# A decode block with cached attention: the first four key loads all in halves, and the projection's second part closed earlier

## The chip, the cores and the metric

One core of a Trainium2 chip runs the whole kernel. The metric is device time in microseconds (us) of that core. Differences here are below one per cent, so most kernels were timed in five or six runs, in alternation with the kernel before on the same chip.

## The reference

```python
xn  = layernorm(x)                              # x: 4 x 1 x 640, bf16
q   = (xn @ wq) per head                        # 32 heads of 128
p   = softmax(q k_cache^T * 128**-0.5)          # caches: 4 x 32 x 4096 x 128, bf16
att = (p v_cache, heads joined) @ wo            # wo: 4096 x 640
mlp = gated MLP of xn                           # w_in 640 x 1728, w_out 864 x 640
return x + att + mlp                            # 4 x 1 x 640
```

The two caches hold 268 MB and are read once. Everything else is small.

## The kernel before

The work is cut into 16 units: four groups of eight heads, times four batch rows. A unit has a K load and a V load of 8.39 MB each. The on-chip buffer has five slots of half a unit, so each load takes two neighbouring slots, and a load can be issued only when what lay there has been read. All large loads go through one queue, in order: K0 to K3, then V0, K4, V1, K5 and so on.

```python
seq = [("k", u) for u in range(B)]                       # B = 4
for u in range(NU):                                      # NU = 16
    seq.append(("v", u))
    if u + B < NU:
        seq.append(("k", u + B))
place = {("k", 0): 3, ("k", 1): 0, ("k", 2): 2, ("k", 3): 0}      # first slot of two
for u in range(B, NU):
    place[("k", u)] = 1 if u % 2 == 0 else 0
for u in range(NU):
    place[("v", u)] = 3
...
cuts = {("k", u): (0, T // 2, T) for u in range(NU) if u == 1 or u % B == B - 1}   # loaded in halves
cuts[("v", NU - 1)] = (0, 128, 192, 240, T)
first = {u: u % 2 for u in range(B, NU) if ("k", u) not in cuts}   # which half is read first
first[2] = 1
```

A K unit is transposed by VectorE in eight pieces, four a half, and multiplied with the queries by TensorE:

```python
hh = first.get(u, 0) ^ (k // 4)                           # half, k = 0..7
nc.vector.transpose(kT[:].rearrange("p (t r) -> p t r", r=32), kw)
... # 8 matmuls into S
```

After the fourth K of a group comes the softmax, then V matmuls of the group. The end of the kernel is the output projection. `proj` is one PSUM bank; even columns c of a group go to its lower rows, odd ones to rows 64 up, and the two parts are added at the end:

```python
odd = c % 2 == 1 and not (g == NG - 1 and c == HG - 1)
r0 = 64 * odd + 32 * hf
nc.tensor.matmul(proj[r0:r0 + B, 0:NO2], lhsT=oT[:, c, :], rhs=wo_t[g][:, c, ...],
                 start=False, stop=(g == NG - 1 and c in (HG - 3, HG - 1)))
...
emit_proj(NG - 1, range(0, HG - 2))
nc.vector.tensor_copy(out=o_1[:], in_=proj[64:128, 0:NO2])
emit_proj(NG - 1, range(HG - 2, HG))
nc.vector.tensor_tensor(out=o_bf[:], in0=proj[0:64, 0:NO2], in1=o_1[:], op=ALU.add)
```

## Time and profile before

| kernel before | |
|---|---|
| time of the three runs at hand for the prediction | 667.51 us median (667.27 to 668.79) |
| the run that was profiled | 668.32 us, span 666.5 |
| DMA over the span | 282.25 MB, 423 GB/s |
| busy: VectorE, TensorE, ScalarE | 54%, 45%, 12% |

The page and the trace's views are read in the prediction below. Two things to know for them: a line of the chain has start, duration and what ran; a line of the queue (SPq) shows when a load was issued, not when its data moved.

### The profile page before, as it was taken

The page shows a single profiled execution, that of the slowest core. Times are in us where ns is not written, and L with a number is a line of the kernel's source. Part 1 is how long each engine was busy: PE and PEld are TensorE (multiplying, and loading weights), DVE is VectorE, ACT ScalarE, POOL GpSimd, SP SyncE. Part 2 cuts the span into 40 slices and gives each one's busy share as a digit, 9 for nine tenths or more (in the row PEclk, how much of TensorE's full clock was granted, in tenths as well). Part 3 has the DMA queues.
Part 4 walks back from the last instruction along what each step waited for, and adds up shares of the span by engine and source line. Part 5 has one row for each costly group of instructions (what it writes and reads, how often), then busy time and mean ns, then how long its engine had stood idle before and what let it go on. Part 6 is the DMA issues. An engine that isn't in the chain of part 4 may idle for free.

```text
span 666.5 us, 5583 instructions
## 1 busy us (share of the span) xinstructions
PE 298.7 (45%) x2366; PEld 110.7 (17%) x2366; DVE 359.2 (54%) x340; ACT 82.7 (12%) x169; POOL 6.2 (1%) x24
## 2 busy tenths in 40 slices
PE   0516466266063446235336065643606254724164
PEld 0402121122021122111112022111202112211021
DVE  5339799555190749609246285735628084940002
ACT  0400000440200000440200000071010000053200
POOL 0000000000000000000000000000000000000000
PEclk9658968668677696766858677755857767667665
DMA  9999999999999999999999999999999999999995
GB/s 374 452 409 462 413 425 438 440 371 440 434 440 438 433 410 444 425 438 437 434 440 425 430 421 441 425 438 440 434 437 426 429 437 416 451 437 426 412 417 224
DMA packets 7381, 282.61 MB, mean 424 GB/s; under 512 B 840, under 2 KB 1212, under 8 KB 1724
## 3 DMA queue, kind: packets, MB, share of 16 engines
q1 hardware_dynamic: 7340, 282.25, 98.5%
q8 instruction: 18, 0.29, 0.2%
q14 instruction: 7, 0.06, 0.0%
q10 hardware_dynamic: 16, 0.01, 0.0%
HBM read 282.25 MB, written 0.01 MB: 423 GB/s over the span
## 4 chain that ended last, share of the span: by engine, by line
DMA 72%; DVE 12%; issue 12%; PE 2%; ACT 1%; SPq 1%; DVEq 0%; ACTq 0%
DMA kv<-in_A_k_cache_dram 64%; DVE kT L353 11%; DMA kv<-in_A_v_cache_dram 4%; DMA kv<-in_A_wo_dram 3%; PE O L435 2%; DVE xd L418 0%; ACT Zb L399 0%; PE S L364 0%; ACT p L407 0%; DVE pT L411 0%; DVE m L371 0%; SPq L152 0%; PE proj L476 0%; SPq L110 0%; PE misc L376 0%
## 5 line engine op out<-in xcount | busy, mean ns | idle before, releaser
L353 DVE STREAM_TRANSPOSE kT<-kv 128x2048 f32<-128x2048 f32 x128 | 282.7, 2277 | 127.2 <-DMA kv<-in_A_k_cache_dram 127.2
L364 PE MATMUL S<-kT,QZ 128*32 128x512 bf16 x1024 | 191.2, 507 | 231.2 <-DVE kT L353 231.2
L364 PEld LDWEIGHTS <-QZ 128*32 128x32 bf16 x1024 | 61.0, 112 | 355.7 <-issue 336.1
L435 PE MATMUL O<-kv,Zb 128*32 128x512 bf16 x1024 | 77.3, 467 | 62.0 <-ACT Zb L399 30.3
L442 DVE TENSOR_SCALAR R<-O,Mk 128x128 f32<-128x128 f32 x16 | 5.6, 351 | 130.8 <-PE O L435 130.8
L399 ACT ACTIVATE Zb<-xd,MkE 32x256 bf16<-32x256 bf16 x112 | 51.5, 499 | 107.2 <-PE O L435 105.8
L407 ACT ACTIVATE p<-S,negmax 128x512 bf16<-128x512 f32 x8 | 5.4, 683 | 402.0 <-DVE negmax L385 402.0
L435 PEld LDWEIGHTS <-Zb 128*32 128x32 bf16 x1024 | 33.2, 114 | 105.2 <-issue 61.5
L452 PE MATMUL misc<-R,SelR 128*32 128x128 f32 x32 | 6.6, 289 | 26.0 <-DVE R L444 26.0
L418 ACT COPY xd<-pT 32x256 bf16<-32x256 bf16 x28 | 17.2, 614 | 5.7 <-DVE pT L411 5.2
L444 DVE SCALAR_TENSOR_TENSOR R<-O,Mk,R 128x128 f32<-128x128 f32 x48 | 16.8, 351 | 1.7
L418 DVE COPY xd<-pT 32x256 bf16<-32x256 bf16 x36 | 13.1, 364 | 0.6
L340 POOL COPY QZ<-q 32x32 bf16<-32x32 bf16 x16 | 5.1, 320 | 424.3 <-PE S L364 398.3
L411 DVE STREAM_TRANSPOSE pT<-p 128x1024 bf16<-128x1024 bf16 x4 | 5.0, 1246 | 6.3 <-ACT p L407 6.3
L476 PE MATMUL proj<-kv,oT 128*4 128x320 bf16 x64 | 6.9, 453 | 2.5 <-DMA kv<-in_A_wo_dram 1.7
L371 DVE TENSOR_REDUCE m<-S 128x2 f32<-128x1024 f32 x4 | 4.9, 1224 | 5.7 <-PE S L364 5.7
L452 PEld LDWEIGHTS misc<-R,SelR 128*32 128x32 f32 x32 | 2.2, 109 | 33.5 <-DVE R L444 24.8
L256 DVE CAST kv<-q 128x512 bf16<-128x512 f32 x4 | 2.5, 684 | 8.4 <-PE q L248 8.4
L376 PE MATMUL misc<-dg,ones_f 128*128 128x256 f32 x8 | 3.6, 537 | 7.6 <-DVE dg L373 7.6
L455 DVE SCALAR_TENSOR_TENSOR om<-misc,rinv,MkH 32x1024 bf16<-32x1024 f32 x4 | 5.1, 1271 | 2.2 <-PE misc L452 2.2
L423 PE MATMUL misc<-rowsum,SelPe 128*32 128x1 f32 x16 | 2.1, 199 | 9.0 <-ACT p L407 9.0
L248 PE MATMUL q<-kv,xnT 128*32 128x512 bf16 x40 | 3.6, 533 | 5.0 <-DMA kv<-in_A_wq_dram 5.0
(94 smaller groups left out, 62.6 us busy)
## 6 DMA issues: line engine op xcount, KB each, us to landing
kv<-in_A_k_cache_dram SPq DMA_DIRECT2D x10, 4096.0 KB, 37.3
kv<-in_A_wq_dram SPq DMA_DIRECT2D x1, 5120.0 KB, 15.2
kv<-in_A_v_cache_dram SPq DMA_DIRECT2D x1, 4096.0 KB
kv<-in_A_wo_dram SPq DMA_DIRECT2D x3, 1280.0 KB, 19.0
kv<-in_B_w_in_dram SPq DMA_DIRECT2D x1, 2160.0 KB, 19.8
kv<-in_A_v_cache_dram SPq DMA_DIRECT2D x1, 2048.0 KB
kv<-in_A_v_cache_dram SPq DMA_DIRECT2D x1, 1536.0 KB
kv<-in_B_w_out_dram SPq DMA_DIRECT2D x1, 960.0 KB
```

Of the source, the lines that this page charges most:

```text
L340: nc.gpsimd.tensor_copy(out=QZ[r0:r0 + 32, :, :, :, 8 + 8 * hp], in_=q3[r0:r0 + 32, :, NE * hp:NE * hp + NE, g * B:g * B + B].rearrange("p ...
L353: nc.vector.transpose(kT[:].rearrange("p (t r) -> p t r", r=32), kw)
L364: nc.tensor.matmul(S_ps[32 * q:32 * q + 32, e], lhsT=QZ[:, b, 2 * kh + w, e, w0:w0 + 32], rhs=kb[:, i, :, e, :, w], start=(b == 0 and k < ...
L399: nc.scalar.activation(out=dst, in_=src, func=ACT.Copy, scale=mk)
L407: nc.scalar.activation(out=p_bf[:, :, e, :], in_=S_ps[:, e], func=ACT.Exp, bias=negmax[:, e:e + 1], scale=scale, accum_out=rowsum[:, e:e + 1])
L418: op(out=xd[32 * hp:32 * hp + 32, :, q, :], in_=pT[32 * q:32 * q + 32, :, hp, :].rearrange("p t x -> p x t"))
L435: nc.tensor.matmul(O_ps[32 * q:32 * q + 32, :, :], lhsT=Zb[b % 2][:, w].rearrange("p h c -> p (h c)"), rhs=vv[:, w * 4 * Dh:(w + 1) * 4 * ...
L442: nc.vector.tensor_scalar(out=R, in0=O_ps[:, 0, :], scalar1=Mk4[:, 0:1], scalar2=None, op0=ALU.mult)
L444: nc.vector.scalar_tensor_tensor(out=R, in0=O_ps[:, c, :], scalar=Mk4[:, c:c + 1], in1=R, op0=ALU.mult, op1=ALU.add)
L452: nc.tensor.matmul(oh[:], lhsT=SelR[:, b].rearrange("p h b -> p (h b)"), rhs=state["R"][:, b, :], start=(b == 0), stop=(b == B - 1))
L455: nc.vector.scalar_tensor_tensor(out=om[:], in0=oh[:, None, :].to_broadcast((G, HG, Dh)), scalar=state.pop(("rinv", g))[:, 0:1], in1=MkH[: ...
L476: nc.tensor.matmul(proj[r0:r0 + B, 0:NO2], lhsT=oT[:, c, :], rhs=wo_t[g][:, c, hf * NO2:(hf + 1) * NO2], start=False, stop=(g == NG - 1 an ...
```

## The change

Its intent: VectorE can start on the first half of K0 sooner, K2 need not land whole, and so the slots of the first group are freed sooner. At the end, the copy of the odd part is taken out of the last matmuls' way by closing that part after column 3.

```diff
-    cuts = {("k", u): (0, T // 2, T) for u in range(NU) if u == 1 or u % B == B - 1}
+    cuts = {("k", u): (0, T // 2, T) for u in range(NU) if u < B or u % B == B - 1}
...
-    first[2] = 1
...
-                odd = c % 2 == 1 and not (g == NG - 1 and c == HG - 1)
+                odd = c % 2 == 1 and not (g == NG - 1 and c >= HG // 2)
...
-                                 start=False, stop=(g == NG - 1 and c in (HG - 3, HG - 1)))
+                                 start=False, stop=(g == NG - 1 and c in (HG // 2 - 1, HG - 1)))
...
-    emit_proj(NG - 1, range(0, HG - 2))
+    emit_proj(NG - 1, range(0, HG // 2))
...
-    emit_proj(NG - 1, range(HG - 2, HG))
+    emit_proj(NG - 1, range(HG // 2, HG))
```

## The prediction

> **What bounds the kernel now.** I first read the page's slices, to see which engine never rests.
>
> ```profile
> DMA  9999999999999999999999999999999999999995
> GB/s 374 452 409 462 413 425 438 440 371 440 434 440 438 433 410 444 425 438 437 434 440 425 430 421 441 425 438 440 434 437 426 429 437 416 451 437 426 412 417 224
> ```
>
> The 16 DMA engines are busy in every slice until the last, and the page has 282.25 MB read in 666.5 us, 423 GB/s. VectorE is busy 54% and TensorE 45%. So only three things can shorten the run: fewer holes in the stream of loads, a shorter start before it or a shorter tail after it. The ninth slice (133 to 150 us) shows 371 GB/s between neighbours at 440: a hole. The first slice is the start-up. A single slice can be off by a few packets that are counted where they end, so I asked for the DMA rate in longer stretches around the hole.
>
> ```profile
> 125.00:137.00 12.00, 4.43 (x42) 1.71 (x46) 5.62 (x15) 9.93 (x19) 0.00 (x0) 0.50 1.00 431
> 137.00:145.00 8.00, 3.14 (x34) 1.21 (x28) 4.52 (x6) 3.62 (x8) 0.00 (x0) 0.71 0.86 330
> 145.00:165.00 20.00, 13.03 (x102) 4.48 (x102) 14.55 (x7) 0.00 (x0) 0.00 (x0) 0.83 0.99 429
> 204.00:640.00 436.00, 192.16 (x1516) 69.94 (x1512) 222.66 (x194) 55.84 (x117) 2.53 (x8) 0.69 1.00 431
> ```
>
> The last two columns are DMA share and GB/s. From 204 to 640 us the rate is 431, so nothing is to be had there. From 137 to 145 us it is 330: 8 us x (431 - 330) / 431 = 1.9 us lost. The stretch before, 117 to 125 us, has 426, another 0.1 us. The DMA packets of the trace, each spread over its own duration, say 0.5 us lost at 118 to 123 and 1.55 at 138 to 145, 2.05 us as a mean of the 16 engines.
>
> A load is usable when the last of the 16 has delivered. The chain of waits shows these moments (start, duration, what):
>
> ```profile
> 82.84 0.05 DVEq L353
> ...
> 115.86 2.30 DVE kT L353
> 118.17 23.70 DMA kv<-in_A_k_cache_dram
> 141.89 2.37 DVE kT L353 x2
> ...
> 150.81 31.55 DMA kv<-in_A_k_cache_dram
> 182.38 2.37 DVE kT L353 x2
> ...
> 191.29 29.71 DMA kv<-in_A_k_cache_dram
> 221.03 2.37 DVE kT L353 x2
> ```
>
> The transposes of K2, K4, K5 and K6 begin at 82.84, 141.89, 182.38 and 221.03 us. K5 to K6 are two units (a V and a K, 8.39 MB each) in 38.65 us: 19.33 us a unit, the undisturbed pitch. K2 to K4 are three units in 59.05 instead of 58.0: 1.05 lost. K4 to K5 are two in 40.49: 1.84 lost. Together **2.9 us lost, all in the first group**. The queue says why:
>
> ```profile
> 91.86 0.33 SPq L144 DMA_DIRECT2D kv<-in_A_v_cache_dram  x1
> 118.17 0.33 SPq L144 DMA_DIRECT2D kv<-in_A_k_cache_dram  x1
> 139.06 0.33 SPq L144 DMA_DIRECT2D kv<-in_A_v_cache_dram  x1
> ```
>
> K4 is issued only at 118.17, when the last transpose of K3 ends and frees its slot, and V0 before it begins to run out on some engines at 119.7 (first completion in the trace). V1 is issued only at 139.06, when V0's matmuls have ended, while K4 is complete on its first engine at 139.3. Both issues come too late by about the time from issue to first data. VectorE is what is late: it starts at 44.06, when all of K0 has landed, works 35.20 us on K0 and K1 without a pause, waits 3.68 us (79.26 to 82.94) for K2, which is one whole load, and works another 35.2 us on K2 and K3.
>
> The end is read in the chain as well:
>
> ```profile
> 661.85 0.04 issue
> 661.89 0.46 PE proj L476 x4
> 662.38 0.50 DVE o L522
> 662.92 0.71 PE proj L476 x4
> 663.66 0.48 DVE o_bf L526
> ```
>
> The output weights are the last load. The copy of the upper half of the projection (0.50 us) stands between the matmuls of columns 4, 5 and those of 6, 7, which wait for it.
>
> **What the Trainium skill says.** "DMA: Bandwidth & Descriptors", section "Where 436 GB/s comes from", gives a ceiling of 435 GB/s for the 16 engines; 431 here is 99% of it, so the trace agrees that the stream is full. "Perfetto Trace Analysis", section "DMA Optimizations", says that splitting a transfer lets parts start sooner and is of use where the DMA engines are generally idle. They are not here; splitting can pay only through the slots that it frees sooner. "DMA: Bandwidth & Descriptors", section "Why a DMA increments its semaphore by 16 and not by 1", says the engines finish independently and only all 16 mean landed; here K4's first completion is at 139.3, its last at 141.9. "PSUM — Partial Sum Buffer", section "PSUM bank collisions raise a hardware error", holds that accesses to different partition quadrants of a bank can coincide, but that guarding by bank is the simple version. The built order has the simple version: the matmul after the copy waits for VectorE, as in the trace (0.6 us).
>
> **The change part by part.** Splitting K0: its first half needs half of 19.33 us less, so it lands at 44.06 - 9.7 = 34.4 us. By then the query tile is ready (GpSimd ends it at 28.4 us) and TensorE is free (33.3). A half unit costs 4 transposes x 2.28 pitched at 2.20 = 8.8 us, less than the 9.7 of its load, so from here VectorE follows the loads:
>
> - K0 34.4 to 43.2 and 44.1 to 52.9; K1 53.8 to 62.6 and 63.5 to 72.3.
> - K2, split too and read from its first half: 73.2 to 82.0 and 82.9 to 91.7. Its second half takes the slot freed at 43.2 and is queued long before its turn.
> - K3 92.5 to 101.3 and 102.2 to 111.0.
>
> V0 must now wait for both halves of K2, no longer one (the reading order of K2 is turned), and can be issued at 91.7, as now (91.86). K4 can be issued at 111.0, 7.1 us sooner and 8.7 ahead of V0's first completion. The softmax and V0's matmuls took from 118.15 to 139.0, 20.9 us; from 111.0 that gives 131.9, so V1 is issued 7.4 us before K4 begins to finish. Both holes close: **-2.9 us** by the last engine, -2.05 by the mean. As the end waits for the last engine and the engines' delays partly even out later, I take **-2.6**.
>
> Against it: K0 and K2 go out in packets of 32 KB, not 64 KB. The trace has 1.215 us for one and 2.418 for the other; 512 x 1.215 - 256 x 2.418 = 3.1 us over 16 engines, **+0.2**. Three more issues of some 0.35 us each stand beside other work; the built queue shows the second half of K0 waiting for a semaphore of the first weight load (landed at 15.9), harmless since its data is due after 34.
>
> The tail: the copy now comes after columns 0 to 3, whose weights land 1.6 us before the last piece (661.0 against 662.6, completions in the trace). Eight matmuls end about 0.85 after their start, the copy takes 0.5, so it ends 0.2 before the last piece lands. But 8 matmuls, not 4, then follow it: about 0.9 us from there (16 took 1.24). The sum starts at 662.6 - 0.1 + 0.9 = 663.4 instead of 663.66: **-0.3**.
>
> Sum: -2.6 + 0.2 - 0.3 = -2.7, and 667.51 - 2.7 = **664.8 us**.
>
> **The rivals.** First, the holes stay: K4 is held by something else than VectorE, or V1 is. For it: a new wait for reused DMA semaphores appears in the queue. Against: those semaphores belong to loads landed long before. Time then: 667.4. Second, the loss counts only as its mean, because the latest engine has other delays: K8 to K9 (301.60 to 341.84) took 40.24 with no late issue, 1.6 over, and that is not touched. Then the gain is 2.0 - 0.2 + 0.3, time 665.4. Third, the split start opens a new hole, or V0 comes late as it waits for all of K2. For it: V0's issue moves by only 0.2. Against: K3 keeps the engines busy to 102. It would cost 1 to 2 us: 666 to 668.
>
> **Range and chances.** The three known runs spread 1.5 us, and one unforced delay costs 1.6. So 663.3 to 667.0. The largest imaginable gain, holes and tail, is 3.5 us or 0.5%, so 2% either way is out of reach.
>
> **What would show it.** First transposes at about 34.4 and K4's issue near 111, V1's near 132, or that step is wrong. K4's transposes should begin at 140.9 or before and K5's at 179.6, not 182.4; the rate at 137 to 145 should read about 431. In the chain's end, no copy between the last matmuls. The prediction fails if the holes close but later steps lose the time again, or if a delay like that at K9 moves.

## The result, and the profile after

| six runs each, same chip | median | lowest to highest |
|---|---|---|
| before | 667.39 us | 667.03 to 668.79 |
| after | 666.12 us | 665.95 to 666.33 |

The ratio is 0.9977, with a 95% interval of 0.9964 to 0.9990. Ratios here are the mean time of one kernel's runs over that of the other's in the same rounds, so not quite the ratio of the medians: the means differ by 1.5 us, the medians by 1.3. The gain is real but half of the 2.7 us foretold. The spread is new as well: 1.8 us before, 0.4 after. The profiled runs were 668.32 and 666.14 us, so the two traces differ by 2.2 us, more than the medians do.

DMA rates from 117 to 145 us, before and then after; the last column is GB/s:

```profile
117.00:145.00 28.00, 11.01 (x90) 4.12 (x86) 13.84 (x27) 15.00 (x31) 1.27 (x4) 0.62 0.96 401
```

```profile
117.00:145.00 28.00, 7.97 (x78) 3.29 (x79) 10.80 (x22) 14.97 (x31) 0.00 (x0) 0.62 1.01 438
```

The hole is filled. The page's slices of the changed kernel agree, where the ninth slice had 371:

```profile
DMA  8999999999999999999999999999999999999995
GB/s 370 427 440 427 424 439 438 439 438 435 435 418 439 427 417 460 422 439 426 423 442 439 430 412 451 434 426 442 431 426 427 434 439 416 461 435 407 425 416 238
```

How VectorE gets there, in order of time in the changed kernel: a row is one half unit, four transposes, with the idle time ahead of it.

```profile
34.48 8.89 DVE L352 STREAM_TRANSPOSE kT<-kv 128x2048 f32<-128x2048 f32 x4 [1.14 <-DMA kv<-in_A_k_cache_dram]
44.29 8.89 DVE L352 STREAM_TRANSPOSE kT<-kv 128x2048 f32<-128x2048 f32 x4 [0.92 <-DMA kv<-in_A_k_cache_dram]
...
83.28 8.89 DVE L352 STREAM_TRANSPOSE kT<-kv 128x2048 f32<-128x2048 f32 x4 [0.83 <-DMA kv<-in_A_k_cache_dram]
92.99 8.89 DVE L352 STREAM_TRANSPOSE kT<-kv 128x2048 f32<-128x2048 f32 x4 [0.82 <-DMA kv<-in_A_k_cache_dram]
102.71 8.89 DVE L352 STREAM_TRANSPOSE kT<-kv 128x2048 f32<-128x2048 f32 x4 [0.84 <-DMA kv<-in_A_k_cache_dram]
```

VectorE now waits 0.8 to 1.1 us for each half: it follows the loads. It ends K3 at 111.6 instead of 118.2, and the queue follows:

```profile
92.19 0.33 SPq L143 DMA_DIRECT2D kv<-in_A_v_cache_dram  x1
111.63 0.33 SPq L143 DMA_DIRECT2D kv<-in_A_k_cache_dram  x1
132.25 0.33 SPq L143 DMA_DIRECT2D kv<-in_A_v_cache_dram  x1
```

K4 is issued 8.4 us before V0 begins to complete (120.0 in the trace), V1 7.1 us before K4 does (139.4). The chain shows the transposes of K4, K5 and K6:

```profile
141.31 2.37 DVE kT L352 x2
...
180.02 2.37 DVE kT L352 x2
...
218.94 2.37 DVE kT L352 x2
```

K4 to K5 takes 38.71 us, the undisturbed pitch, where it was 40.49. K5 comes 2.36 us sooner than in the trace before. The end of the chain:

```profile
658.71 0.04 issue
658.75 0.73 PE proj L475 x8
659.48 0.02 issue
659.51 0.50 DVE o L521
660.01 0.04 issue
660.05 1.25 PE proj L475 x8
661.30 0.02 issue
661.32 0.48 DVE o_bf L525
```

There still is a copy between the matmuls. It starts sooner against the last landing (660.3 in the trace, 662.6 before), but the matmuls after it take 1.25 us where they took 0.71. The last sum starts 1.02 us after the last landing, as it did before (663.66 against 662.64). The 1.06 in an expectation below is what the landing rounded to 662.6 gives.

### The profile page after: what moved, and what is told of

The parts are those of the page before. It is cut to its first block, busy times and chain, and to the rows that moved or that the text cites. A ratio compares the mean times of both kernels' runs of the same rounds, so it can differ in the third digit from the quotient of the medians.

```text
span 664.3 us, 5584 instructions
## 1 busy us (share of the span) xinstructions
PE 300.6 (45%) x2366; PEld 110.9 (17%) x2366; DVE 359.9 (54%) x340; ACT 82.6 (12%) x169; POOL 6.2 (1%) x24
## 4 chain that ended last, share of the span: by engine, by line
DMA 75%; issue 10%; DVE 10%; PE 3%; ACT 1%; SPq 0%; DVEq 0%; ACTq 0%
DMA kv<-in_A_k_cache_dram 64%; DVE kT L352 9%; DMA kv<-in_A_v_cache_dram 5%; DMA kv<-in_A_wo_dram 3%; DMA kv<-in_A_wq_dram 2%; PE O L434 2%; PE q L247 1%; DVE xd L417 0%; DVE kv L255 0%; ACT Zb L398 0%; PE proj L475 0%; ACT kv L255 0%; ACT p L406 0%; PE misc L278 0%; DVE pT L410 0%
## 5 line engine op out<-in xcount | busy, mean ns | idle before, releaser
L363 PE MATMUL S<-kT,QZ 128*32 128x512 bf16 x1024 | 197.8, 522 | 227.1 <-DVE kT L352 227.1
L363 PEld LDWEIGHTS <-QZ 128*32 128x32 bf16 x1024 | 62.5, 114 | 356.8 <-issue 340.1
L434 PE MATMUL O<-kv,Zb 128*32 128x512 bf16 x1024 | 72.5, 444 | 61.3 <-ACT Zb L398 30.2
```

The lines of the kernel that those rows point to most:

```text
L363: nc.tensor.matmul(S_ps[32 * q:32 * q + 32, e], lhsT=QZ[:, b, 2 * kh + w, e, w0:w0 + 32], rhs=kb[:, i, :, e, :, w], start=(b == 0 and k < ...
L434: nc.tensor.matmul(O_ps[32 * q:32 * q + 32, :, :], lhsT=Zb[b % 2][:, w].rearrange("p h c -> p (h c)"), rhs=vv[:, w * 4 * Dh:(w + 1) * 4 * ...
```

## The experiments

The theory after the result, called A: the loads give all of the gain, by closing the holes before K4 and V1; the tail gives nothing. The rivals are told with each run. For the traces I also add up the "hole": the bytes of each DMA packet spread over its own duration, and the shortfall from 96 to 170 us against the same trace's rate from 200 to 630 us (432.3 to 432.5 GB/s), in us. For the trace before it gives 1.99, for the changed kernel none.

### The loads alone, and the tail alone

The first has the changed loads with the old tail; the second the old loads with the changed tail. Each is one half of the diff above.

> All four first K loads in two, the tail as before. Theory A (the two holes in the load stream are closed, the tail gives nothing because eight matmuls in two row groups take 1.25 us): nearly the whole gain of the change, 1.2 to 1.6 us under before, holes at 118 to 145 us gone, V1 issued near 132. Rival B (the tail gives 0.3 as predicted): only about 1.0 to 1.2 us under before. Rival C (gain comes from somewhere else than the loads): as before.

> Loads as before, the projection's second part closed after column 3. Theory A: no gain, within 0.15 us of before; the copy ends 0.3 us before the last weights land, then eight matmuls of 1.25 us; the sum starts 1.0 us after the last landing, as before (1.06). Rival B: 0.3 us under before.

| | median | lowest to highest | ratio to before, 95% |
|---|---|---|---|
| before (11 runs) | 666.72 us | 665.84 to 668.62 | |
| loads only (5) | 666.08 | 666.01 to 666.22 | 0.9990, 0.9977 to 1.0003 |
| tail only (5) | 667.15 | 666.29 to 667.88 | 1.0004, 0.9992 to 1.0017 |

The kernel with the loads alone has the time and the tightness of the changed kernel, to within 0.05 us. The tail alone is as before. On this chip the kernel before had a lower mean (666.92 us) than in the runs of the result (667.64), so the interval of the loads-only kernel includes 1. With runs 3 us apart on one chip, that difference between the two sets can be chance. What makes the kernel before scatter became the question of the later runs. The tail alone could not be judged by its time to the 0.15 us that I had asked for, as it inherits the spread of the kernel before. The traces do judge it: the last sum starts 0.98 us after the last landing with the new tail and 0.99 with the old one (loads only).

### K2 alone, and K0 alone

```diff
 # K2 alone                                       # (and first[2] = 1 taken out)
-... if u == 1 or u % B == B - 1}
+... if u in (1, 2) or u % B == B - 1}
 # K0 alone                                       # (first[2] = 1 stays)
+... if u in (0, 1) or u % B == B - 1}
```

> Only K2 in two (read from its first half), K0 whole, tail as before. Theory A: VectorE starts at 44 us, has no pause before K2 (79.3 instead of 82.9), ends K3 at about 114.6, K4 is issued there and V1 near 135.5, both in time: no hole, 1.2 to 1.7 us under before, as good as splitting all or 0.1 better (256 fewer small packets). Rival D (the early start with half of K0 is what counts): half the gain or none, V1 issued late, a hole at 138 to 145.

> Only K0 in two, K2 whole and read from its second half, tail as before. Theory A: VectorE starts at 34.4 us but loses it all waiting for the whole of K2 until 82.9; K3 ends at 118 and K4 and V1 are issued at 118 and 139 as before: both holes stay, time as before or up to 0.2 more (smaller packets). Rival D: most of the gain, 1.0 to 1.5 us under before.

| same chip and rounds as those two | median | lowest to highest | ratio to before, 95% |
|---|---|---|---|
| K2 alone (5) | 666.11 us | 665.88 to 666.17 | 0.9990, 0.9978 to 1.0002 |
| K0 alone (6) | 667.62 | 665.93 to 668.17 | 1.0009, 0.9997 to 1.0021 |

VectorE and the queue with K2 alone in halves:

```profile
44.46 70.29 DVE L352 STREAM_TRANSPOSE kT<-kv 128x2048 f32<-128x2048 f32 x32 [11.54 <-DMA kv<-in_A_k_cache_dram]
```

```profile
114.78 0.33 SPq L143 DMA_DIRECT2D kv<-in_A_k_cache_dram  x1
135.09 0.33 SPq L143 DMA_DIRECT2D kv<-in_A_v_cache_dram  x1
```

And with K0 alone:

```profile
34.46 8.89 DVE L353 STREAM_TRANSPOSE kT<-kv 128x2048 f32<-128x2048 f32 x4 [1.56 <-DMA kv<-in_A_k_cache_dram]
...
83.05 35.20 DVE L353 STREAM_TRANSPOSE kT<-kv 128x2048 f32<-128x2048 f32 x16 [10.47 <-DMA kv<-in_A_k_cache_dram]
```

```profile
118.28 0.33 SPq L144 DMA_DIRECT2D kv<-in_A_k_cache_dram  x1
138.34 0.33 SPq L144 DMA_DIRECT2D kv<-in_A_v_cache_dram  x1
```

The interval of K2 alone against the kernel before still includes 1; against K0 alone, in the same rounds, it is 1.3 us faster on the mean (666.05 against 667.36). With K2 alone VectorE starts as late as before but runs its 32 transposes in one go, and the 3.7 us that K2's late landing had cost are enough: both loads are issued in time and there is no hole. With K0 alone VectorE starts 9.6 us sooner, waits 10.47 us for K2, and issues nothing sooner. So the early start, the striking part of the change, adds nothing by itself; the split of K2 does it.

### Is there one deadline?

One line is taken out of the kernel before: `first[2] = 1`. K2, still one load, is now read from its first half, and V0 must wait for all of it.

> The kernel before with one line out: K2 is read from its first half, so V0 must wait for all of K2. V0 is then issued near 100.6 us instead of 91.9, when the engines are just ending K3 (first completion 100.4): a new hole of some 2 us at 100 to 104. Theory A' (what counts is one deadline, the issue of V1 near 139; idle time before it is taken from the holes that come anyway): K4 and V1 stay at 118 and 139, the holes at 118 and 138 shrink, time as before within 0.6 us (before: 665.8 to 668.8, mean 667.2). Rival E (holes add up): 2 us over before.

Measured: 666.97 us median (666.67 to 667.11, 6 runs) against 667.34 (665.64 to 668.82, 11 runs); ratio 0.9994 (0.9982 to 1.0005). Its queue and its DMA rate from 100 to 117 us:

```profile
100.82 0.33 SPq L143 DMA_DIRECT2D kv<-in_A_v_cache_dram  x1
118.36 0.33 SPq L143 DMA_DIRECT2D kv<-in_A_k_cache_dram  x1
138.42 0.33 SPq L143 DMA_DIRECT2D kv<-in_A_v_cache_dram  x1
```

```profile
100.00:117.00 17.00, 10.09 (x66) 3.40 (x64) 17.00 (x9) 0.00 (x0) 0.00 (x0) 0.90 0.93 386
```

A hole of 1.94 us opened at 100 us as foreseen, and those at 118 and 138 shrank to 0.2 in all. The sum is 2.09, within the 1.0 to 2.6 us of the traces without the new hole (table below). Holes do not add up here: until V1 is issued near 138, the engines can move only what was issued before, and it matters little where in that time they stand still. No run issues V1 early while K4 is still late, so what the hole before K4 costs alone stays open.

### A delay put in on purpose

```diff
-        nc.vector.tensor_reduce(out=m1[:], in_=S_ps[:]..., axis=AX.X, op=ALU.max)
+        for _ in range(3 if g == 0 else 1):
+            nc.vector.tensor_reduce(out=m1[:], in_=S_ps[:]..., axis=AX.X, op=ALU.max)
```

> The kernel before with the first max over the scores of group 0 done three times (two more reductions of 1.22 us on VectorE, 2.45 us, same result). Theory A' (V1's issue has no slack in the kernel before): V1 is issued near 141.5, the hole grows and the time by 1.7 to 2.7 us over before. Rival F (the start of the first group has slack, the gain came otherwise): as before.

> The same two extra reductions in the changed kernel. Theory A': V1 is issued near 134.7 instead of 132.25, still well ahead of K4's first completion at 139.4: no hole, 666.1 as the changed kernel without them, and tight as it (0.4 us from lowest to highest). Rival F: 2 us more.

| same chip and rounds as the run before | median | lowest to highest | ratio to before, 95% |
|---|---|---|---|
| before with the delay (6) | 668.36 us | 667.50 to 668.81 | 1.0014, 1.0002 to 1.0027 |
| after with the delay (6) | 666.12 | 665.91 to 666.35 | 0.9982, 0.9970 to 0.9995 |

The rows of the queue for V1, before with the delay and after with it:

```profile
141.48 0.33 SPq L144 DMA_DIRECT2D kv<-in_A_v_cache_dram  x1
```

```profile
134.68 0.33 SPq L143 DMA_DIRECT2D kv<-in_A_v_cache_dram  x1
```

The delay reaches V1's issue in both. In the changed kernel it costs nothing: it has slack there. In the kernel before it costs time, which shows that V1's issue sets it; but 1.1 us on the means (668.31 against 667.22), not the 1.7 to 2.7 that I expected. The hole grew to 3.60 us.

### The tail with a second bank

In the changed kernel the matmuls of columns 4 and 5 wait for the copy, though they write other rows of the bank. Here columns 4 to 7 go to a bank of their own, and the two parts of the first bank are added while the last weights land.

```diff
+    proj2 = ps_j.tile([P, 512], F32, name="proj2")
+    nc.vector.memset(proj2[0:64, 0:NO2], 0.0)
...
-                nc.tensor.matmul(proj[r0:r0 + B, 0:NO2], lhsT=oT[:, c, :],
+                nc.tensor.matmul((proj2 if late else proj)[r0:r0 + B, 0:NO2], lhsT=oT[:, c, :],
...                                                    # late: last group, c >= HG // 2; starts a new sum
+    o_2 = const.tile([64, NO2], F32)
+    nc.vector.tensor_tensor(out=o_2[:], in0=proj[0:64, 0:NO2], in1=o_1[:], op=ALU.add)
     emit_proj(NG - 1, range(HG // 2, HG))
-    ... in0=proj[0:64, 0:NO2], in1=o_1[:], op=ALU.add)
+    ... in0=proj2[0:64, 0:NO2], in1=o_2[:], op=ALU.add)
```

> The changed kernel with columns 4 to 7 of the last group summed in a second PSUM bank, so that they need not wait for the copy out of the first; the two halves of the first bank are added meanwhile. Expected if the copy's wait is what spoils the tail: columns 4 and 5 run on landing, after the last landing one pair of matmuls (0.47) is left, the last sum starts 0.55 instead of 1.02 us after the last landing: 0.4 to 0.5 us under the changed kernel, 665.6 to 665.7. If the tail is bound by TensorE however it is arranged: 666.1.

Measured: 665.64 us median (665.59 to 665.83, 6 runs); ratio to before 0.9975 (0.9963 to 0.9986). The delayed changed kernel in the same rounds had 666.12. Its chain ends:

```profile
659.46 1.27 PE proj L478 x8
660.73 0.02 issue
660.75 0.48 DVE o_bf L531
```

The eight matmuls still span 1.27 us, but they run while weights land and the copy is off the chain. The last sum starts 0.51 us after the last landing (660.24), where I had expected 0.55, and 0.47 us are gained.

### K2 alone with the second bank, and the kernel before twice more

> Only K2 in two, K0 whole, with the tail in two banks. If splitting K0 adds nothing and the second bank's gain is independent of it: 665.6 to 665.7, as with all four split (665.64), tight.

Measured: **665.45 us** median (665.33 to 665.71, 5 runs); ratio to before 0.9973 (0.9959 to 0.9986). This is the fastest, by 0.2 us over all four in halves with the second bank, though the two ran on different chips and that difference is not settled.

> The kernel before once more, for a second trace of its holes. If the holes cost what the last engine loses and not their mean size: the mean idle time at 118 to 145 us is again about 2 us, but the last completion of V1 (163.0 in the trace on record) varies by some 2 us between runs (161 to 163) and the time with it, 665.6 to 668.8.

> As the run before it: a third trace of the same kernel, holes of about 2 us on the mean, a last completion of V1 anywhere from 161 to 163, the time with it.

The two looks had 667.72 and 668.55 us. With all traces in which K3 ends at 118, and those without a hole in the last row:

| trace | V1 issued | hole, us | mean landing of the last weights | last engine behind it | time of that run |
|---|---|---|---|---|---|
| tail only | 137.76 | 1.02 | 658.5 | 3.4 | 667.50 |
| K0 alone | 138.34 | 1.11 | 658.5 | 1.7 | 665.93 |
| order of K2 | 138.42 | 2.09 | 659.7 | 1.7 | 667.11 |
| before, on record | 139.06 | 1.99 | 659.4 | 3.2 | 668.32 |
| before, third trace | 139.43 | 2.55 | 660.2 | 2.7 | 668.55 |
| before, second trace | 140.18 | 2.43 | 660.2 | 1.9 | 667.72 |
| before with delay | 141.48 | 3.60 | 661.3 | 1.6 | 668.64 |
| loads only, K2 alone, changed, changed with delay | 132.3 to 135.1 | none | 657.7 to 658.0 | 2.4 to 2.7 | 665.91 to 666.17 |

The mean landing is that of the 16 DMA engines for the last piece of the output weights, from the semaphore updates in the trace; the column after it tells how much later the last of the 16 delivers.

My expectation that the mean idle time is about 2 us in every run, and only the last engine's share varies, was half wrong: the hole itself varies, 1.0 to 2.6 us over the kernels without the delay, 2.0 to 2.6 in the three traces of the kernel before. The other half held: the last completion of V1 was 163.0, 162.8 and 163.8 in those three, and in the eleven traces with the tail in one bank the time of the run is 504.5 to 505.5 us more than that completion. Part of the scatter comes from V1's issue, and some of that from V0's matmuls: start and duration in the traces before, second of before, and tail only:

```profile
132.80 6.21 PE L435 MATMUL O<-kv,Zb 128*32 128x512 bf16 x64 [7.57 <-ACT Zb L399]
```

```profile
133.71 6.42 PE L435 MATMUL O<-kv,Zb 128*32 128x512 bf16 x64 [7.56 <-ACT Zb L399]
```

```profile
132.37 5.34 PE L435 MATMUL O<-kv,Zb 128*32 128x512 bf16 x64 [7.56 <-ACT Zb L399]
```

The same 64 matmuls took 5.34 to 6.42 us, and they started up to 1.3 us apart. While they ran, the granted clock was 0.67 in the tail-only trace and 0.58 and 0.56 in the other two; duration times granted clock is 3.5 to 3.6 us in nine traces, each read over the stretch of these matmuls. Without slack this goes into V1's issue; with 7 us of slack it costs nothing. That fits the spread: 37 timed runs of the kernel before lie between 665.64 and 668.82 us, 22 of the four kernels without a hole between 665.88 and 666.35.

## Why the prediction was right or wrong

The measured 666.12 us lies in the range and "within 2%" was right. The range is 3.7 us wide and ends 0.4 us under the time before, so to lie in it says little. By its steps:

- **The timeline of VectorE and the queue was right.** Predicted were the first transposes at 34.4, K4's issue at 111.0, V1's at 131.9, K4's transposes by 140.9 and K5's at 179.6; found were 34.5, 111.6, 132.3, 141.3 and 180.0, the last two 0.4 us late.
- **The holes closed**, as foretold, and no new one opened. The first rival (they stay) and the third (a new hole, V0 late) fell. V0's issue moved by 0.3 us and was in time.
- **The step that failed is the term "-2.6".** It took the loss read from one trace as the loss of the median run. The loads are worth 1.1 us on the means of all runs on all chips (667.20 before in 37 runs, 666.10 without a hole in 22), 1.5 in the six runs of the result. Two things were mis-sized. First, the profiled run was itself one of the longer ones: 668.32 us against a median of 667.51, which stood in the numbers at hand. For that trace the term was nearly right: the last output weights landed 2.33 us sooner in the changed kernel (660.31 for 662.64), against 2.6 - 0.2 foretold. Second, the extra loss of the last engine over the mean (2.9 against 2.05) was taken from that one trace too, and it varies from run to run. The second rival, that the loss counts only by its mean (665.4), was nearer than the main line and still too large.
- **What takes up the rest** is how far the last engine ends behind the mean of the 16 (last table). Without a hole the mean landing is about 657.8 us; holes of 1.0 to 3.6 us move it by 0.7 to 3.6, so the idle time is lost nearly whole. But the run ends with the last engine, 2.4 to 2.7 us behind the mean without a hole and 1.6 to 3.4 with one. So a hole of 1.02 us went with a run of 667.50 us and one of 1.11 with 665.93, and the profiled run before had both a hole and a last engine far behind. Why the last engine falls behind in some runs and catches up in others stays open.
- **Small packets, "+0.2":** not resolved. V0's last completion was 121.9 us in the changed kernel, and 121.6 to 122.0 in the three traces of the kernel before.
- **Two readings of the prediction are off, without effect on its sum.** The row at 82.84 is VectorE's queue, and the transposes of K2 begin at 82.94; the 1.05 us lost holds between the landings (82.82 and 141.87). The rates of slices and stretches count a packet where it starts, not where it ends.
- **The tail, "-0.3", was wrong**; the sum starts 1.02 us after the last landing, as before, and the sign named for it, no copy between the last matmuls, failed. The eight matmuls behind the copy were sized by 16 that took 1.24 us and put at 0.9; they took 1.25. Those 16 lie on four row groups of the bank. Columns 4 to 7 all go to the even part, so on two groups, and the trace starts a pair every 0.22 to 0.27 us against four in that time; no run varied the row groups alone. The copy was sized right (0.50), and with the second bank, where nothing waits for it, the tail did give 0.47.

## What to carry to other kernels

In a kernel bound by loads, look for the load whose issue has no slack against the end of the load before it, and find what frees its slot; splitting pays where it frees that slot sooner, and a split elsewhere (K0) may look busier and bring nothing. Weigh a hole by several runs and not by one trace: compare the profiled run with the median first, and the last engine with the mean of the 16. When matmuls are moved behind another step, size them by matmuls of the same row groups.

## What the Trainium skill lacked or had wrong

- "Perfetto Trace Analysis", section "DMA Optimizations", offers splitting where the DMA engines are generally idle. Here they were busy throughout but for 2 us, and the split of one load (K2) took the mean from 667.20 us (37 runs before) to 666.05 (5 runs), because it frees buffer slots sooner. The page lacks that case.
- "DMA: Bandwidth & Descriptors", section "Bandwidth", speaks of the rate of whole transfers. I found no page that says that the first packets take longer once the engines have run dry: the first sixteen of 64 KB after the hole at 139 us took 2.70 to 3.69 us in the trace, the usual one 2.42.
- "DMA: Bandwidth & Descriptors", section "Why a DMA increments its semaphore by 16 and not by 1", says that the engines finish independently, but not how far apart: 1.8 us for K0 (42.2 to 44.0) in a stream that was full, and 3.4 to 5.5 us for the last output weights.
- "PSUM — Partial Sum Buffer", section "PSUM bank collisions raise a hardware error", calls guarding by bank the simple version. The runs show a price for it: 0.47 us at the end of this kernel, gained back with a second bank.
